# First row chunk of a SiLU feed-forward backward pass: four groups of h side by side over row slices of w1, x transposed in pairs

## Chip, cores, metric

One Trainium2 chip, one core. The metric is the device time of one execution in microseconds (us). The span in a profile is the profiled part of it; it is 1.7 to 2.0 us shorter than the time here.

## The reference, cut

```python
def _fwd_reference(x, w1, w2):          # x [1,2048,640], w1 [640,1536], w2 [1536,640], bfloat16
    h = jnp.einsum("bsd,df->bsf", x, w1)
    h = jax.nn.silu(h)
    return jnp.einsum("bsf,fd->bsd", h, w2)

def reference(x, w1, w2, grad_out):     # the output, and the gradients of x, w1, w2
    out, vjp = jax.vjp(_fwd_reference, x, w1, w2)
    return (out, *vjp(grad_out))
```

## The kernel before

The 2048 rows go in four chunks of 512. For a chunk, TensorE computes h transposed in 12 groups of 128 columns of w1, each a sum over five row blocks of 128 ("dt"). ScalarE and VectorE make silu and its derivative. Then come the down-projection, the gradient of the activation, the gradient of x, and after the last chunk the two weight gradients. Only the start of the first chunk matters here: x and w1 are loaded, x is transposed on TensorE through PSUM, and h begins.

```python
        load_x_tile(nc.sync, 0)
        load_x_tile(nc.scalar, 1)
        load_x_tile(nc.sync, 2)
        load_x_tile(nc.scalar, 3)
        for lo, hi in ((0, 2), (2, DT)):                      # FH = 256 columns
            nc.sync.dma_start(out=w1_nat[:, lo:hi, 0:FH], in_=w1_v[:, lo:hi, 0:FH])
        load_w1(FH, FC)                                       # columns 256..511
        for fc in range(1, NFC):                              # columns 512..1023, 1024..1535
            load_w1(fc * FC, (fc + 1) * FC)
        # ... loads of w2, transposing loads of grad_out, w2, w1 (cut)
        def pe_x_tile(xT, st):
            for lo, hi, copy in ((0, DS, nc.vector.tensor_copy), (DS, DT, nc.scalar.copy)):   # DS = 3
                tp = ps_h.tile([P, hi - lo, P], dt_in, name="tp", tag="hp")
                for dt_ in range(lo, hi):
                    nc.tensor.transpose(tp[:, dt_ - lo, :], x_nat[:, st, dt_ * P:(dt_ + 1) * P], ident[:])
                copy(out=xT[:, lo:hi, st * P:(st + 1) * P], in_=tp[:])
        for st in range(STC):
            pe_x_tile(xT_next, st)
        for i in range(NFILL):                                # 4 fills, reading the last x tile (cut)
            nc.tensor.matmul(wp[:, 0:P], lhsT=ident[:], rhs=x_nat[:, STC - 1, 0:P], start=True, stop=True)
        def h_group(ft, xT, aT, ghT):
            hp = ps_h.tile([P, SC], FP32, name="hp")          # 8 PSUM buffers in all
            for dt_ in range(DT):
                nc.tensor.matmul(hp[:], lhsT=w1_nat[:, dt_, ft * P:(ft + 1) * P], rhs=xT[:, dt_, :],
                                 start=(dt_ == 0), stop=(dt_ == DT - 1))
            # silu to aT, tanh, two VectorE steps to ghT (cut)
        # ... first chunk:
                for ft in range(FT):
                    h_group(ft, xT, aT, ghT)
```

Before all this, 26 matmuls on a constant run from launch until x arrives, so that the TensorE clock is raised early.

## Time and profile before

| | before |
|---|---|
| median of the three executions | 321.93 us (321.66 to 322.12) |
| span of the profiled execution | 320.5 us |
| first h matmul | 6.48 us |
| first matmul of the down-projection (60 h matmuls later) | 19.43 us |

From the page of the kernel before: span, TensorE's busy time with its share and number of instructions, the chain that ended last by engine, and the group of h matmuls (busy us, mean ns of one, idle before them and what ended it).

```profile
span 320.5 us, 3556 instructions
...
PE 314.0 (98%) x1477; PEld 145.9 (46%) x1506; DVE 101.8 (32%) x179; ACT 78.6 (25%) x142; POOL 0.7 (0%) x6
...
PE 97%; DMA 1%; issue 1%; ACT 0%; SPq 0%; DVE 0%; DVEq 0%
...
L161 PE MATMUL hp<-xT,w_nat 128*128 128x512 bf16 x232 | 56.4, 379 | 0.6 <-ACT xT L149 0.2
```

TensorE is the whole story: 98% busy, 97% of the chain. As the change keeps TensorE's matmuls, the time can only come down where TensorE waits. The timeline of the first 20 us (start, duration, engine, line, operation, output<-inputs, count, and in brackets the idle time before it and its releaser):

```profile
0.78 2.93 PE L96 MATMUL wp<-const-bfloat16-1.0 128*128 128x128 bf16 x26 [0.78 <-PEq L362]
...
3.62 0.74 PE L148 MATMUL tp<-ident,x_nat 128*128 128x128 bf16 x10
...
5.32 0.73 PE L148 MATMUL tp<-ident,x_nat 128*128 128x128 bf16 x10 [0.96 <-DMA x_nat<-in_x_dram]
...
5.81 0.65 ACT L149 COPY xT<-tp 128x256 bf16<-128x256 bf16 x2 [1.04 <-PE tp L148]
...
6.48 13.11 PE L161 MATMUL hp<-xT,w_nat 128*128 128x512 bf16 x58 [0.21 <-ACT xT L149]
7.75 0.60 ACT L168 ACTIVATE aT<-hp 128x512 bf16<-128x512 f32 x1 [1.30 <-PE hp L161]
...
19.43 10.74 PE L196 MATMUL hp<-aT,w_nat 128*128 128x512 bf16 x48
```

The reader sees the warm-up, two rounds of ten transposes, the last copy of transposed x (ScalarE, ending near 6.46), and then h without a break up to 19.43: 12.95 us for 60 matmuls, 0.216 us each. All that TensorE waits for in this execution (us in total, times, longest):

```profile
PE tp L148 <- DMA x_nat<-in_x_dram: 1.0, 1, 1.0
PE wp L96 <- PEq L362: 0.8, 1, 0.8
PE hp L161 <- ACT xT L149: 0.2, 1, 0.2
```

```profile
w_nat<-in_w_dram SPq DMA_DIRECT2D x1, 640.0 KB, 6.5
```

Issued at 1.16 and 1.19, the tiles land at 5.50 and 5.27 us. Issued at 3.16, the second block lands at 9.65, and the fifth group, its first reader, starts 20 matmuls after 6.48, at 10.80: a margin of 1.1 us in this one execution. (Landing times to the hundredth here and below are the trace's own records of each transfer.)

### The profile page before, as it was taken

What the parts mean: (1) busy time and instruction counts of PE and PEld (TensorE: products, weight loads), DVE (VectorE), ACT (ScalarE), POOL (GpSimd) and SP (SyncE); (2) the same over time, 40 slices, a digit from 0 to 9 for tenths busy, and PEclk for the clock granted to TensorE, in tenths of its full rate; (3) what the DMA queues carried; (4) which work ended last, traced back from release to release, by engine and by line L of the source; (5) the groups of instructions that cost most, each with busy time, mean ns of one, the idle gap of its engine ahead of it and who ended that gap; (6) DMA issues with size and microseconds to landing.
All of it is one profiled execution on the core that took longest, in us unless ns stands there. A gap on an engine that the chain in (4) does not pass through costs nothing.

```text
span 320.5 us, 3556 instructions
## 1 busy us (share of the span) xinstructions
PE 314.0 (98%) x1477; PEld 145.9 (46%) x1506; DVE 101.8 (32%) x179; ACT 78.6 (25%) x142; POOL 0.7 (0%) x6
## 2 busy tenths in 40 slices
PE   7999999999999999999999999999999999999996
PEld 5444444444444444444444444444444444444443
DVE  1871551477510087810147741000000100001001
ACT  3960001555201255411054520110100001001100
POOL 0000000000000000000000000000000000000000
PEclk9999999999999999999999999999999999999999
DMA  8999999999699884392445079819999999995011
GB/s 246 316 192 209 254 265 253 320 271 277 215 229 336 203 237 122 118 319 66 127 159 141 2 254 268 217 25 293 262 240 263 249 203 343 251 281 181 33 49 35
DMA packets 149264, 66.69 MB, mean 208 GB/s; under 512 B 112640, under 2 KB 149248, under 8 KB 149248
## 3 DMA queue, kind: packets, MB, share of 16 engines
q1 hardware_dynamic: 148960, 66.13, 80.8%
q10 hardware_dynamic: 288, 0.33, 0.3%
q8 instruction: 12, 0.20, 0.2%
q14 instruction: 4, 0.03, 0.0%
HBM read 9.18 MB, written 28.97 MB: 119 GB/s over the span
## 4 chain that ended last, share of the span: by engine, by line
PE 97%; DMA 1%; issue 1%; ACT 0%; SPq 0%; DVE 0%; DVEq 0%
PE hp L196 32%; PE hp L180 16%; PE hp L286 16%; PE hp L161 16%; PE hp L334 15%; DMA x_nat<-in_x_dram 1%; PE hp L316 1%; ACT xT L149 0%; PE tp L148 0%; SPq L123 0%; DVE g_2366 L327 0%; DVEq L327 0%
## 5 line engine op out<-in xcount | busy, mean ns | idle before, releaser
L161 PE MATMUL hp<-xT,w_nat 128*128 128x512 bf16 x232 | 56.4, 379 | 0.6 <-ACT xT L149 0.2
L180 PE MATMUL hp<-goT,w2T 128*128 128x512 bf16 x238 | 56.8, 379 | 0.1
L196 PE MATMUL hp<-aT,w_nat 128*128 128x512 bf16 x235 | 52.2, 379 | 0.3
L196 PE MATMUL hp<-ghT,w1T 128*128 128x512 bf16 x235 | 52.2, 379 | 0.3
L286 PE MATMUL hp<-a_blk,go_nat 128*128 128x512 bf16 x236 | 51.8, 379 | 0.2
L334 PE MATMUL hp<-gh_blk,x_nat 128*128 128x512 bf16 x219 | 48.2, 379 | 0.3
L204 ACT ACTIVATE oT<-hp 128x512 bf16<-128x512 f32 x24 | 14.3, 597 | 110.0 <-PE hp L196 110.0
L168 ACT ACTIVATE aT<-hp 128x512 bf16<-128x512 f32 x48 | 28.7, 597 | 31.7 <-PE hp L161 31.7
L196 PEld LDWEIGHTS <-w_nat 128*128 128x128 bf16 x240 | 23.5, 98 | 28.3
L180 PEld LDWEIGHTS <-w2T 128*128 128x128 bf16 x240 | 23.5, 98 | 28.3
L286 PEld LDWEIGHTS <-go_nat 128*128 128x128 bf16 x240 | 23.5, 98 | 28.3
L161 PEld LDWEIGHTS <-w_nat 128*128 128x128 bf16 x240 | 23.4, 98 | 28.4 <-issue 0.4
L196 PEld LDWEIGHTS <-w1T 128*128 128x128 bf16 x240 | 23.4, 98 | 28.4
L206 DVE CAST oT<-hp 128x512 bf16<-128x512 f32 x16 | 11.1, 692 | 78.0 <-PE hp L196 78.0
L187 DVE SCALAR_TENSOR_TENSOR ghT<-ghT,hp 128x512 bf16<-128x512 bf16 x48 | 32.5, 682 | 7.3 <-PE hp L180 7.3
L334 PEld LDWEIGHTS <-x_nat 128*128 128x128 bf16 x224 | 21.9, 98 | 26.4
L173 DVE SCALAR_TENSOR_TENSOR ghT<-aT,v 128x512 bf16<-128x512 bf16 x48 | 33.0, 688 | 0.6
L172 DVE TENSOR_SCALAR v<-t 128x512 bf16<-128x512 f32 x48 | 20.5, 427 | 29.2 <-ACT t L170 29.2
L170 ACT ACTIVATE t<-hp 128x512 f32<-128x512 f32 x48 | 28.4, 591 | 0.0
L296 DVE CAST g2T<-hp 128x512 bf16<-128x512 f32 x7 | 4.8, 692 | 46.1 <-PE hp L286 46.1
L294 ACT ACTIVATE g2T<-hp 128x512 bf16<-128x512 f32 x8 | 4.8, 598 | 47.0 <-PE hp L286 40.7
L343 ACT ACTIVATE g_2140<-hp 128x512 bf16<-128x512 f32 x1 | 0.6, 597 | 13.6 <-DMA out_dram<-g_2077 13.6
(33 smaller groups left out, 29.3 us busy)
## 6 DMA issues: line engine op xcount, KB each, us to landing
aT_scr<-aT SPq DMA_DIRECT2D x4, 1536.0 KB, 6.7
ghT_scr<-ghT SPq DMA_DIRECT2D x4, 1536.0 KB, 8.0
out_dram<-o_sb SPq DMA_DIRECT2D x8, 640.0 KB, 3.4
oT_scr<-oT SPq DMA_DIRECT2D x4, 640.0 KB, 3.9
go_nat<-in_grad_out_dram SPq DMA_DIRECT2D x4, 640.0 KB, 8.1
gxT_scr<-oT SPq DMA_DIRECT2D x4, 640.0 KB, 4.7
w_nat<-in_w_dram SPq DMA_DIRECT2D x2, 960.0 KB, 10.9
x_nat<-in_x_dram SPq DMA_DIRECT2D x3, 640.0 KB, 7.8
```

What stands on the lines that cost most here:

```text
L161: nc.tensor.matmul(hp[:], lhsT=w1_nat[:, dt_, ft * P:(ft + 1) * P], rhs=xT[:, dt_, :], start=(dt_ == 0), stop=(dt_ == DT - 1),)
L168: nc.scalar.activation(aT[:, ft, :], hp[:], ACT.Silu)
L170: nc.scalar.activation(t[:], hp[:], ACT.Tanh, scale=0.5)
L172: nc.vector.tensor_scalar(out=v[:], in0=t[:], scalar1=-0.5, scalar2=0.5, op0=ALU.mult, op1=ALU.add)
L173: nc.vector.scalar_tensor_tensor(out=ghT[:, ft, :], in0=aT[:, ft, :], scalar=1.0, in1=v[:], op0=ALU.subtract, op1=ALU.mult)
L180: nc.tensor.matmul(gp[:], lhsT=w2T[:, dt_, ft * P:(ft + 1) * P], rhs=goT[:, dt_, :], start=(dt_ == 0), stop=(dt_ == DT - 1),)
L187: nc.vector.scalar_tensor_tensor(out=ghT[:, ft, :], in0=ghT[:, ft, :], scalar=1.0, in1=gp[:], op0=ALU.add, op1=ALU.mult)
L196: nc.tensor.matmul(op_[:], lhsT=w_all[:, ft, dt_ * P:(dt_ + 1) * P], rhs=rhs_all[:, ft, :], start=(ft == 0), stop=(ft == FT - 1),)
L204: nc.scalar.activation(oT[:, dt_, :], op_[:], ACT.Copy)
L206: nc.vector.tensor_copy(out=oT[:, dt_, :], in_=op_[:])
L286: nc.tensor.matmul(gp[:], lhsT=go_nat[:, st, dt_ * P:(dt_ + 1) * P], rhs=a_blk[:, st, :], start=(st == 0), stop=(st == ST - 1),)
L334: nc.tensor.matmul(gp[:], lhsT=x_nat[:, st, dt_ * P:(dt_ + 1) * P], rhs=gh_blk[:, st, :], start=(st == 0), stop=(st == ST - 1),)
```

## The change

The intent: let h start as soon as the first row block of x is transposed and the first row slice of w1 is there, and feed it slice by slice: four groups share a slice, so four matmuls run per 128 KB. The queues and the order of the x loads are not changed by this diff.

```diff
-        for lo, hi in ((0, 2), (2, DT)):
-            nc.sync.dma_start(out=w1_nat[:, lo:hi, 0:FH], in_=w1_v[:, lo:hi, 0:FH])
-        load_w1(FH, FC)
+        for lo, hi in ((0, 1), (1, 2), (2, 3), (3, DT)):
+            nc.sync.dma_start(out=w1_nat[:, lo:hi, 0:FC], in_=w1_v[:, lo:hi, 0:FC])
         for fc in range(1, NFC):
             load_w1(fc * FC, (fc + 1) * FC)
 ...
+        def pe_x_pair(xT, st):
+            for dt_ in range(DT):
+                tp = ps_h.tile([P, 2, P], dt_in, name="tp", tag="hp")
+                for q in range(2):
+                    nc.tensor.transpose(tp[:, q, :], x_nat[:, st + q, dt_ * P:(dt_ + 1) * P], ident[:])
+                copy = nc.scalar.copy if dt_ % 2 else nc.vector.tensor_copy
+                copy(out=xT[:, dt_, st * P:(st + 2) * P], in_=tp[:])
+        pe_x_pair(xT_next, 0)
         for i in range(NFILL):
-            nc.tensor.matmul(wp[:, 0:P], lhsT=ident[:], rhs=x_nat[:, STC - 1, 0:P], ...)
+            nc.tensor.matmul(wp[:, 0:P], lhsT=warm, rhs=warm, start=True, stop=True)
+        pe_x_pair(xT_next, 2)
 ...
+        def h_first(xT, aT, ghT):                       # FB = 4, KM = 3, LAG_G = 4
+            hps = []
+            for ft in range(FB):
+                hps.append(ps_h.tile([P, SC], FP32, name="hp"))
+            for dt_ in range(KM):
+                for ft in range(FB):
+                    h_mm(hps[ft], ft, xT, dt_, dt_ + 1)
+            for i in range(FT + LAG_G):
+                if i < FT:
+                    if i < FB:
+                        h_mm(hps[i], i, xT, KM, DT)
+                    else:
+                        hps.append(ps_h.tile([P, SC], FP32, name="hp"))
+                        h_mm(hps[i], i, xT, 0, DT)
+                    silu_a(i, hps[i], aT)
+                if i >= LAG_G:
+                    silu_grad(i - LAG_G, hps[i - LAG_G], aT, ghT)
 ...
-                for ft in range(FT):
-                    h_group(ft, xT, aT, ghT)
+                h_first(xT, aT, ghT)
```

## The prediction

> **What bounds the kernel now.** TensorE. The page shows PE busy 314.0 of 320.5 us (98%) at full granted clock; the chain that ended last is 97% PE. In the timeline h runs from 6.48 to 19.43 us: 60 matmuls at 0.216 us, no gap. That is the warm gap for 512 columns in the Trainium skill, "TensorE: Matmul & The Clock Gate", section "Back-to-back issue gap"; the trace agrees. The waits view lists no later PE wait worth naming. Only the head (0 to 6.48) and the tail are not matmul-bound, and the change touches the head alone.
>
> **What sets the head.** By the landings in the trace, x tiles 0 to 3 land at 3.57, 3.74, 5.27 and 5.50 us. The last ten transposes issue from 5.32 to 5.83 (0.056 apart), four fills follow, and the last copy (ScalarE, 0.373 us) ends at 6.46. The first h matmul waits for it. w1 is not the gate: its first three pieces land at 5.78, 6.43 and 7.39, before use.
>
> **What the change does.**
> - The x loads stay as they are, queues and order. No gain.
> - w1's first 512 columns come as rows 0, 1, 2, 3-4. At the observed rate (192 KB in 0.65 us) I estimate landings near 5.8, 6.2, 6.6 and 7.4; four groups side by side need them at 6.1, 7.0, 7.8 and 8.7. It removes a w1 wait that the trace doesn't have. The next block landed at 9.65 and will be needed near 10.4; its issue moves back 0.4 us. Tight, but it holds.
> - Transposes in pairs by row block: the first h matmul needs only block 0 of all four tiles. The second transpose waits for tile 3, so nine run from 5.55 to 6.05. The copy of block 0 (VectorE, 256 columns; estimated 0.29 us from 0.358 at 384) runs 5.81 to 6.10. The other copies end before 6.7, ahead of need.
> - The fills no longer read x; the compiled order puts them behind the warm-up: off the critical path, before and after.
> - Silu of four groups first, tanh and gradient four groups later: ScalarE's 24 activations (about 13 us at their 0.54 us spacing) start near 9.3 instead of 7.75 and end near 22.5 instead of 20.7. The gradient is not used until about 32; the last silu (19.9) comes before its matmul (21.4). PSUM buffers are held longer, but eight suffice.
>
> **On the critical path:** first h matmul near 6.12 instead of 6.48: 0.36 us. The matmul count is unchanged; the rest just shifts.
>
> **Predicted time: 321.6 us, range 321.0 to 322.2.** Faster by over 2%: 0.01; within 2%: 0.98; slower: 0.01.
>
> **Right or wrong in the profile:** first h matmul between 6.0 and 6.3; its releaser a VectorE copy of xT, not w1; 60 h matmuls still in 12.95 us, no PE wait at the fifth group; ScalarE idle until about 9.3; PE busy near 314; span about 320.1.
>
> **What would make it wrong:** w1's next block landing after 10.4 (a stall of some tenths); x tile 3 slowed by the larger w1 runs; the TensorE clock, raised at 3.67 us in this trace, dropping or rising late because the fills moved (1 to 2 us); a later DMA-released stage that does not move forward with the matmuls, so that the gain is given back.

## More of the kernel before

The transfers whose issue falls in a window (KB each, us from issue to landing): x tiles 3 and 2 first, then w1's second block, columns 512 to 1023.

```profile
x_nat<-in_x_dram ACTq DMA_DIRECT2D x1, 160.0 KB, 4.3
x_nat<-in_x_dram SPq DMA_DIRECT2D x1, 160.0 KB, 4.1
```

## The result, and the profile after

The changed kernel took 322.48 us in the median of four executions (321.83 to 322.83), the kernel before 321.80 (321.54 to 322.12). The ratio is 1.0018, 95% interval 1.0000 to 1.0037. Ratios are computed from means: the mean time of one kernel's fast runs over that of the other's of the same rounds, so a ratio is not quite that of the medians quoted. The forecast was 321.6 with a range up to 322.2, so the measured median lies above the range. The class, within 2%, was right, but that was never in doubt.

The same lines of the page after:

```profile
span 320.7 us, 3592 instructions
...
PE 315.9 (98%) x1506; PEld 145.9 (45%) x1506; DVE 101.1 (32%) x181; ACT 77.8 (24%) x142; POOL 0.7 (0%) x6
...
PE 96%; DMA 3%; DVE 0%; issue 0%; DVEq 0%
...
L158 PE MATMUL hp<-xT,w_nat 128*128 128x512 bf16 x240 | 57.2, 379 | 1.2 <-DMA w_nat<-in_w_dram 1.2
```

```profile
3.50 0.50 PE L153 MATMUL wp<-const-bfloat16-1.0 128*128 128x128 bf16 x4
...
3.84 1.52 PE L147 MATMUL tp<-ident,x_nat 128*128 128x128 bf16 x20
4.15 1.54 DVE L149 COPY xT<-tp 128x256 bf16<-128x256 bf16 x6 [4.15 <-PE tp L147]
...
5.30 4.64 PE L158 MATMUL hp<-xT,w_nat 128*128 128x512 bf16 x20
...
8.68 2.06 ACT L167 ACTIVATE aT<-hp 128x512 bf16<-128x512 f32 x4 [2.97 <-PE hp L158]
...
11.13 8.81 PE L158 MATMUL hp<-xT,w_nat 128*128 128x512 bf16 x40 [1.19 <-DMA w_nat<-in_w_dram]
...
19.77 10.52 PE L221 MATMUL hp<-aT,w_nat 128*128 128x512 bf16 x48
```

```profile
PE hp L158 <- DMA w_nat<-in_w_dram: 1.2, 1, 1.2
PE wp L99 <- PEq L385: 0.8, 1, 0.8
```

```profile
x_nat<-in_x_dram ACTq DMA_DIRECT2D x1, 160.0 KB, 3.5
x_nat<-in_x_dram SPq DMA_DIRECT2D x1, 160.0 KB, 3.2
```

```profile
w_nat<-in_w_dram SPq DMA_DIRECT2D x1, 640.0 KB, 7.3
```

The head became much shorter than forecast: the first h matmul starts at 5.30 instead of 6.48. Most of that is not the pairing: x tiles 2 and 3 landed after 3.2 and 3.5 us instead of 4.1 and 4.3, so the last of them came 0.86 us earlier (4.64 instead of 5.50); the other 0.32 us lie between that landing and the first h matmul. But 20 matmuls later TensorE waits for w1's second block, which landed at 11.08 us, 7.3 after its issue, not 6.5. The bracket says 1.19 us, counted from the modelled end of the matmul before; from start to start it is 1.57, less the usual 0.22, so 1.35 us lost. Row slice 1 of w1 cost another 0.15 (landed at 6.27, needed at 6.16). The sum closes: 1.18 won, 1.35 + 0.15 lost, and the down-projection starts at 19.77 instead of 19.43, 0.34 later (0.32 by the sum). From there to the end of the span both kernels take the same: 300.9 us after, 301.0 before.

So the trace shows a new wait that eats a larger gain than was forecast. It is one execution, though. Are both figures, the early x and the late w1, the change's doing?

### The profile page after: what moved, and what is told of

It is laid out like the page before. It is cut to its first block, busy times and chain, and to the rows that moved or that the text cites. A ratio compares the mean times of both kernels' runs of the same rounds, so it can differ in the third digit from the quotient of the medians.

```text
span 320.7 us, 3592 instructions
## 1 busy us (share of the span) xinstructions
PE 315.9 (98%) x1506; PEld 145.9 (45%) x1506; DVE 101.1 (32%) x181; ACT 77.8 (24%) x142; POOL 0.7 (0%) x6
## 4 chain that ended last, share of the span: by engine, by line
PE 96%; DMA 3%; DVE 0%; issue 0%; DVEq 0%
PE hp L221 32%; PE hp L309 16%; PE hp L205 16%; PE hp L357 15%; PE hp L158 15%; DMA w_nat<-in_w_dram 2%; PE hp L339 1%; DMA x_nat<-in_x_dram 1%; DVE g L350 0%; DVEq L350 0%
## 5 line engine op out<-in xcount | busy, mean ns | idle before, releaser
L158 PE MATMUL hp<-xT,w_nat 128*128 128x512 bf16 x240 | 57.2, 379 | 1.2 <-DMA w_nat<-in_w_dram 1.2
L231 DVE CAST oT<-hp 128x512 bf16<-128x512 f32 x16 | 11.1, 692 | 76.2 <-PE hp L221 76.2
L368 DVE CAST g<-hp 128x512 bf16<-128x512 f32 x7 | 4.8, 692 | 47.0 <-PE hp L357 26.7
```

What stands on the lines that cost most here:

```text
L231: nc.vector.tensor_copy(out=oT[:, dt_, :], in_=op_[:])
```

## The experiments

Theory A: the earlier start leaves the second block too little time, so the gain in the head is paid back at the fifth group. Rival B: that wait was one execution's accident and the time goes elsewhere (silu starting later, PSUM held longer). Kernels are compared only within the same rounds.

### The two kernels again: a_again, b_again, a_again2, a_again3

No edit.

> The changed kernel unchanged, for a second trace and more rounds. Theory A (the head got about 1.2 us shorter, and the fifth group then waits for w1's second block, columns 512 to 1023): the first h matmul starts near 5.3 us again, the second block lands near 11 us again, TensorE waits 1 to 1.5 us before the fifth group, ratio to before 1.000 to 1.003. Rival B (the late landing was an accident of one execution, and the time is lost elsewhere): the second block lands near 9.7, no wait of TensorE, and the ratio is still near 1.002.

> The kernel before, unchanged, for a second trace and as a null comparison: ratio 1.000 within 0.1%. If x tiles 2 and 3 land near 5.3 and 5.5 us again, their earlier landing in the changed kernel (4.4 and 4.6) belongs to the change (theory A1: w1's larger runs behind them disturb them less); if they land near 4.5 here too, it is chance from one execution to the next (A2).

> The changed kernel once more, for a third trace beside its split version on another chip. Theory A: ratio to before 0.999 to 1.002; if the second block of w1 lands later than 4.3 us after the first h matmul, TensorE waits for exactly the difference. Rival F (the slow executions come from a late raise of the TensorE clock instead): a slow trace shows the clock raised after 6.2 us and h matmuls 0.43 us apart, as the slow execution of b_reuse did.

> A fourth trace of the changed kernel: long packets 4 us or more between 4 and 9 us (8.8, 9.8 and 10.3 so far); the fifth group waits by as much as the second block lands later than 4.3 us after the first h matmul (1.35, 0 and 0.3 us so far).

Measured: b_again 1.0000 (0.9988 to 1.0012). The changed kernel 0.9995 (0.9980 to 1.0009; 321.45 to 323.00 in six runs) and 0.9983 (0.9970 to 0.9996) on another chip, below what was expected there. a_again3 is one run: 321.53 beside 322.22 of before. The traces, in us; "needed" is the first h matmul plus 20 spacings of 0.2158 (12.95 us over 60):

| trace | last x tile lands | clock raised | first h | second block lands | needed | lost at fifth group | down-projection |
|---|---|---|---|---|---|---|---|
| before | 5.50 | 3.67 | 6.48 | 9.65 | 10.80 | 0 | 19.43 |
| b_again | 4.76 | 5.27 | 6.06 | 10.46 | 10.38 | 0.13 | 19.15 |
| changed | 4.64 | 3.73 | 5.30 | 11.08 | 9.77* | 1.35 | 19.77 |
| a_again | 4.71 | 5.49 | 5.79 | 9.27 | 10.11 | 0 | 18.74 |
| a_again2 | 4.60 | 4.39 | 5.90 | 10.49 | 10.22 | 0.30 | 19.18 |
| a_again3 | 4.54 | 4.84 | 5.67 | 9.98 | 9.99 | 0.05 | 18.67 |

(* with the 0.15 us lost at row 1 added.) The timeline of TensorE for the start and end of h, in a_again (nothing late) and in a_again2:

```profile
5.79 13.11 PE L158 MATMUL hp<-xT,w_nat 128*128 128x512 bf16 x58
18.74 1.46 PE L221 MATMUL hp<-aT,w_nat 128*128 128x512 bf16 x6
```

```profile
5.90 13.44 PE L158 MATMUL hp<-xT,w_nat 128*128 128x512 bf16 x58 [0.47 <-DMA w_nat<-in_w_dram]
19.18 1.03 PE L221 MATMUL hp<-aT,w_nat 128*128 128x512 bf16 x4
```

In a_again2 the first h matmul itself was released by w1's first slice (landed at 5.86), not by a copy of x.

What follows. The early landing of x is not the change's alone: it came early in b_again too, with the old loads, so chance (A2) is enough for it. Over all 18 traces, though, the last x tile landed after 5 us only with the old w1 pieces (before, and b_reuse below: two of four traces, against none of fourteen with the new ones). So A1, that the new pieces disturb x less, may hold for a part and stays open. The second block's landing scatters as well, 9.3 to 11.1 us for one and the same program; with the old loads it was 9.2 to 10.5 in four traces, so that the change itself makes it later is not shown. But the same lateness costs the two kernels different amounts, because the changed one needs the block up to 1 us earlier: the block at 10.46 cost b_again 0.13, at 10.49 it cost a_again2 0.30, and at 11.08 it cost 1.35. Where nothing was late (a_again), the span is 319.7. So A's wait exists but not in every execution. Whether the first four executions were a bad draw or that call was a slower one is not shown: its interval (1.0000 to 1.0037) does not meet that of a_again2 (0.9970 to 0.9996), the calls ran on different chips where the chip is recorded, and for the first it is not.

The pairing itself can be read from the distance between the last x tile's landing and the first h matmul. With the clock raised before the last transposes it is 0.98 before and 0.66 in the changed trace; with the clock raised later, 1.30 (b_again) and 1.08 (a_again). That is 0.2 to 0.3 us, close to the 0.36 forecast. Other traces below, with the clock raised before the last transposes, agree: 0.98 with the old transposes (b_w1rows2), 0.71 with pairs (a_split2, a_halves).

### Taking the wait away: a_reuse, and the same in the kernel before: b_reuse

```diff
-                        h_mm(hps[i], i, xT, 0, DT)
+                        h_mm(hps[i], i - FB if i < 2 * FB else i, xT, 0, DT)
```

Groups 4 to 7 of the first chunk read w1's first 512 columns, which landed long before; the result is wrong (relative error 0.41), work and loads are the same. b_reuse does the same in the kernel before, by an argument of `h_group`.

> Wrong result on purpose: groups 4 to 7 of the first row chunk read w1's columns 0 to 511 again, so that nothing needs the second block before group 8. Same work, same loads. Theory A: the wait of about 1.3 us is gone, the down-projection starts near 18.3 instead of 19.8 us, ratio to before 0.996 (about 320.6 us). Rival B: the ratio stays near 1.002.

> Wrong result on purpose: the kernel before with groups 4 to 7 of the first chunk reading w1's columns 0 to 511 again, so that it never waits for the second block. Theory A says that before rarely waits there (0 and 0.13 us in its two traces): ratio 0.999 to 1.000. If it gains as much as the changed kernel did by the same step (0.2%), that wait was always there and is not a price of the change.

Measured: a_reuse 0.9978 (0.9965 to 0.9990), against 0.9995 of a_again: means 321.47 and 321.96. So an estimate of what the wait costs the changed kernel is 0.5 us on average; with five and six executions of this scatter (95%: 0.5 ± 0.7) the difference is not clear of noise. The gain over the kernel before is, but it was half of what was expected from the one bad trace, as the wait is not always 1.35. In its trace the second block landed at 10.24 and no wait is left; the down-projection started at 19.02, not 18.3, since the clock was raised only at 6.06 and the transposes ran slowly:

```profile
6.06 13.12 PE L158 MATMUL hp<-xT,w_nat 128*128 128x512 bf16 x58
19.02 1.24 PE L221 MATMUL hp<-aT,w_nat 128*128 128x512 bf16 x5
```

b_reuse gained nothing: 1.0013 (0.9995 to 1.0030). So the wait is a price of the change, not one that was there before: rival B falls.

b_reuse's interval is wide because of its first run, 323.85 us, the one that was profiled. TensorE's timeline in it:

```profile
3.74 1.25 PE L148 MATMUL tp<-ident,x_nat 128*128 128x128 bf16 x10
5.68 1.25 PE L148 MATMUL tp<-ident,x_nat 128*128 128x128 bf16 x10 [0.70 <-DMA x_nat<-in_x_dram]
...
7.26 5.09 PE L162 MATMUL hp<-xT,w_nat 128*128 128x512 bf16 x19
```

The h matmuls stand 0.43 us apart up to 8.97 us, where the trace records the raise of the TensorE clock; in the other traces it came between 3.5 and 6.1. The Trainium skill, "TensorE: Matmul & The Clock Gate", Part 1 ("What's actually happening"), says that the clock is raised after a busy window of about 3.4 us, and that the window runs freely, so that the raise depends on where in it the matmuls begin. A scatter agrees with that, and so do the records: in all 18 traces the time from one change of the clock to the next is a whole multiple of 3.413 us. It is the third random quantity of the head (rival F): here the first four h matmuls lost about 0.8 us by it (0.38 to 0.43 us each instead of 0.216). Together with a late x (5.88 us) it made this execution 1.9 us longer than the mean of its five neighbours, in a kernel with the old head. Whether the changed kernel's 323.00 us run was of this kind, no trace tells.

### A smaller first piece: a_split, a_split2, a_best

```diff
-        for fc in range(1, NFC):
-            load_w1(fc * FC, (fc + 1) * FC)
+        load_w1(FC, FC + FC // 2)
+        load_w1(FC + FC // 2, 2 * FC)
+        load_w1(2 * FC, F)
```

a_best has, besides, three row slices instead of four: `((0, 1), (1, KM), (KM, DT))`.

> The second block of w1 comes as two halves of 256 columns, so the fifth group needs 320 KB less. Theory A: the wait before the fifth group shrinks to 0 to 0.4 us, as the first half lands about 1 us before the whole did; ratio 0.996 to 0.998. Rival B: no change, near 1.002.

> The split second block once more. Theory A: no wait at the fifth group, ratio 0.997 to 0.999 and 0.001 to 0.002 below the changed kernel beside it. If it equals the changed kernel within 0.0005, the first result was chance.

> Three row slices instead of four, and the second block in two halves. Theory A: as a_split2, 0.997 to 0.999; no additional gain from the earlier issue.

Measured: a_split 0.9979 (0.9966 to 0.9991), a_split2 on another chip 0.9977 (0.9965 to 0.9989), a_best 0.9982 (0.9970 to 0.9994), all correct. The means lie 0.51 us (a_split), 0.26 us (a_split2) and 0.10 us (a_best) below the changed kernel; the second is 0.0008 of it, a bit less than the 0.001 that was expected. None of the three differences is clear of noise (95%: ± 0.7, 0.4 and 0.5). TensorE's timelines of a_split and a_split2, start and end of h:

```profile
5.69 13.11 PE L159 MATMUL hp<-xT,w_nat 128*128 128x512 bf16 x58
18.64 1.67 PE L222 MATMUL hp<-aT,w_nat 128*128 128x512 bf16 x7
```

```profile
5.69 13.11 PE L159 MATMUL hp<-xT,w_nat 128*128 128x512 bf16 x58
18.63 1.67 PE L222 MATMUL hp<-aT,w_nat 128*128 128x512 bf16 x7
```

The fifth group's half landed at 8.49 and 8.37 us, needed at 10.0; no wait for w1 is left in either trace. a_split has the lowest mean of the correct kernels: ten executions on two chips, 320.97 to 322.03, mean 321.41. It gains 0.7 us, 0.2%, on the kernel before, clear of noise; that it also beats the changed kernel is likely (0.4 us, 95%: ± 0.4) and not settled. Three slices instead of four make no measurable difference.

### Making the wait longer: a_swap

```diff
-        for fc in range(1, NFC):
+        for fc in range(NFC - 1, 0, -1):
```

> The changed kernel with the second block of w1 queued behind the third: the suspected wait made about 2 us longer (the third block landed 1.9 us after the second in every trace). Theory A: the fifth group waits in every execution, 1.2 to 3.3 us; the down-projection starts near 20 to 21.5 us; ratio to the changed kernel 1.004 to 1.006. If something off this path set the time, less than 1.002.

Measured: 323.04 to 326.00 us in six runs, ratio to before 1.0069 (1.0042 to 1.0097). Against the mean of a_again2 beside it, 321.64, the mean of 324.35 is a ratio of 1.0084; the four runs with full granted clock have a mean of 323.57, a ratio of 1.0060; 1.004 to 1.006 was expected. Its trace is of one of the other two (granted clock 0.994):

```profile
5.99 4.48 PE L158 MATMUL hp<-xT,w_nat 128*128 128x512 bf16 x19
13.07 10.31 PE L158 MATMUL hp<-xT,w_nat 128*128 128x512 bf16 x39 [2.60 <-DMA w_nat<-in_w_dram]
23.22 1.03 PE L221 MATMUL hp<-aT,w_nat 128*128 128x512 bf16 x4
```

TensorE waited 2.60 us, and the 60 h matmuls took 17.2 us instead of 13: besides the wait, the matmuls after 13.07 ran at half rate, as the trace records the clock lowered at 12.74 and raised again at 16.15. The down-projection starts at 23.22, later than the 20 to 21.5 expected, for this second cost. So a late second block is paid in full, as A says, and a wait of this length can be paid a second time through the clock.

### The parts of the change by themselves: b_pairs, b_w1rows, b_w1rows2

b_pairs is the kernel before with `pe_x_pair` and the new fills, b_w1rows the kernel before with the four row slices (the first and second hunk of the diff above).

> The kernel before with the changed transposes alone (pairs by row block, fills behind the warm-up; old w1 pieces, old group order). Theory A (pairing shortens the head by about 0.3 us between tile 3's landing and the first h matmul; the other two parts are not needed for that): first h matmul 0.7 to 1.0 us after tile 3's landing where the clock has been raised by then, instead of 1.0 to 1.3; ratio 0.998 to 0.999, with waits for w1 now and then. Rival C (only the side-by-side order with row slices makes the earlier start usable): the second w1 piece, rows 2 to 4, is late for the third matmul, the wait eats the gain, ratio 1.000.

> The kernel before with the changed w1 loads alone (four row slices of 512 columns; old transposes, old group order). The first group then needs all four slices at once. If slices of one row block make the transfers stumble more (theory D): packets over 150 ns add up to 8 us or more between 4 and 9 us, as in three of the four traces of the changed loads, against 2.4 to 3.3 in the two of before, and the second block lands after 10 us. If not (chance): about 2 to 4 us. Time: ratio 1.000 to 1.003, as the first group waits some tenths for rows 3 and 4.

> A second trace of the kernel before with the sliced loads: long packets again above 4 us if the loads cause them (the first had 6.6), below 3.3 if that was chance.

Measured: b_pairs 0.9998 (0.9986 to 1.0010). In its trace the first h matmul starts 1.14 us after the last x tile (clock raised late, at 5.33), no wait, span 319.8; but its five runs do not show the gain. That fits rival C, that an earlier start alone is not usable with the old w1 pieces, but no trace of it shows that wait, so it stays open. b_w1rows: 1.0018 (1.0006 to 1.0030), slower, as expected. The reason expected was that the first group alone needs all four slices; the first trace, of the fastest of the five runs, has no such wait, and the second (b_w1rows2, one run) has it:

```profile
PE hp L160 <- DMA w_nat<-in_w_dram: 1.6, 2, 1.3
```

So slices without the side-by-side groups are a loss. That the side-by-side order is what makes them bearable is argued from this wait; no run has the order changed alone. Of theory D's two numbers b_w1rows met neither: 6.6 us of long packets instead of 8 or more, and a second block at 9.43 instead of after 10; b_w1rows2 met both (8.6 and 10.20).

### Issue time and the shape of the w1 transfers: a_three, a_one, a_halves

a_three is the changed kernel with three slices, so that the second block is the eighth transfer and not the ninth. In the changed trace the issue of the ninth waits for an x tile to land (tile 1, at 3.80, not tile 0 as the expectation says) and comes at 3.81; here it comes at 3.14. a_one loads the 512 columns in one transfer, `load_w1(0, FC)`; a_halves loads each slice in two halves of 256 columns.

> The changed kernel with three slices instead of four (row 0, rows 1 and 2, rows 3 and 4), so that the second block's issue does not wait for tile 0's completion and comes at about 3.1 us as before, not 3.8. If the later issue delays the block (theory E): it lands by about 0.5 us earlier and the ratio is 0.998. If the queue was never empty and issue time is immaterial: as the changed kernel, 0.9995 to 1.001, with or without a wait at the fifth group.

> For its trace alone: the changed kernel with w1's first 512 columns in one transfer of five row blocks (1 KB runs, no slices). If slicing by row block makes the transfers stumble (D1), packets over 150 ns between 4 and 9 us add up to 1.5 to 3.3 us, as in the four traces of the old order. If the 1 KB runs do (D2), to 4 us or more, as in the ten with slices. The first h matmul then waits for the whole block, near 7.3 us, so about 1.5 us slower.

> For its trace alone: the same row slices, each as two transfers of 256 columns (512 B runs as in the kernel before). D1 (slices): long packets add up to 4 us or more between 4 and 9 us. D2 (run length): 1.5 to 3.3 us.

Measured: a_three 0.9994 (0.9981 to 1.0007), the second block at 9.21, close to the earliest of the changed kernel's four (9.27 to 11.08); the ratio of 0.998 that theory E asks for did not come, so it is not supported. a_one: one run, 325.37 beside 322.22; the block came at 8.34 and TensorE waited 3.0 us for it. It landed 1 us later than expected, and the clock went down during the wait, as in a_swap: the trace records it lowered at 7.71 and raised at 11.13, with h matmuls 0.43 us apart in between. So it lost more than the 1.5 us expected. a_halves: one run, 322.42; the second block at 11.10, 1.0 us of wait by the waits view.

Why the block is late can be followed one step further. A 1 KB packet usually takes 0.05 us. In the changed trace three took 0.89, 1.24 and 1.73 us, from 4.47, 5.75 and 6.95 us on, nearly end to end; this looks like one DMA engine standing still most of the time from 4.5 to 8.7 us, though the records of packets don't name the engine. The Trainium skill, "DMA: Bandwidth & Descriptors", section "Why a DMA increments its semaphore by 16 and not by 1", says that a transfer counts as landed only when every engine that takes part has finished its share; the block landing at 11.08, while the others went on moving the next loads, agrees with that. The trace also records the sixteen steps, by that section one for each engine, in which a transfer's semaphore rises. In the changed trace fifteen of the second block's steps had come by 9.63 us, before the need at 9.77, and the last alone came at 11.08. In the four traces of the changed kernel half of the steps had come by 8.3 to 9.1, and the last lagged the fifteenth by 1.45, 0.03, 0.43 and 0.83 us. The late x tiles look the same: tile 3 had fifteen steps by 4.95 (before) and 4.73 (b_reuse) and the last at 5.50 and 5.88. In all four traces of the table with a loss at the fifth group the fifteenth step came before the need. So it was one late share of sixteen that made these waits, and the late x.

Packets over 0.15 us between 4 and 9 us add up, beyond 0.05 us each, to this:

| loads of w1 | traces | us |
|---|---|---|
| old pieces | before, b_again, b_pairs, b_reuse | 1.5 to 3.3 |
| four slices, second block whole | changed, a_again, a_again2, a_again3, a_reuse, a_swap, b_w1rows, b_w1rows2 | 6.6 to 10.3 |
| slices, second block in halves | a_split, a_split2, a_best | 3.7 to 5.7 |
| three slices | a_three | 5.7 |
| one transfer | a_one | 4.0 |
| slices in halves | a_halves | 7.7 |

So the new loads do stumble more (theory D), and less with the second block in halves, so a_split may help in two ways. But this sum does not tell when the block lands: a_again has 9.8 us of long packets and the earliest landing of the four (9.27), b_again 3.3 and 10.46. Neither explanation of the long packets holds alone, by one trace each: a_one is above the old range, against D1, and a_halves as well, against D2. What makes one share late remains open.

## Why the prediction was right or wrong

- **What bounds the kernel, what sets the head.** Right. TensorE's time after the first chunk's h is the same in every trace, 300.9 to 301.0 us, and only the head moved. One caution on the prediction's citation: its section gives 0.216 us as the gap of an isolated matmul, and about 0.131 us for a stream of weight loads and matmuls with 512 columns. h is such a stream and took 0.216, so the trace agrees with the formula and not with that second figure.
- **Pairing is worth 0.36 us.** Nearly right: 0.2 to 0.3 us between the last x tile and the first h matmul. The forecast start, 6.12, was missed (5.30 to 5.90) because it took x's landing at 5.50 from one trace; 4.5 to 5.0 is the usual value in this kernel's traces.
- **w1's slices arrive with slack everywhere.** Not always: a_again2's first h matmul waited for slice 0, and row 1 cost 0.15 us in the changed trace.
- **"The next block landed at 9.65 and will be needed near 10.4 ... Tight, but it holds."** This is the step that failed. The need moved to 9.8 to 10.2, and the landing is not a constant: 9.27 to 11.08 in four traces of the same program. In the changed trace the need came 0.7 us earlier than forecast (9.77, not 10.4) and the landing 1.4 us later (11.08, not 9.65), for the last of its sixteen shares. The loss was 1.35, 0, 0.30 and 0.05 us, 0.4 on average; the runs with the wait removed or eased (a_reuse, a_split, a_split2) give an estimate of 0.3 to 0.5 us, not clear of noise one by one. The prediction counted 0. It named this stall among its risks but gave it "some tenths", and its range reached 0.6 us above the forecast, less than half of what the first trace lost.
- **Silu first, tanh later, PSUM held longer: free.** Right; a_split has all of that and no wait.
- **The fills' move and the clock.** The clock's raise does vary by some us, but in the kernel before too; no trace ties it to the fills.
- **The time.** 321.6 forecast, 322.48 measured. Over all sixteen executions of the changed kernel the mean is 321.94, with a standard deviation of 0.53, against 322.10 and 0.29 for the 27 of the kernel before. In executions where the second block is late the fifth group gives the head's gain back, in part or whole: with the wait removed or eased the changed kernel is 0.2% faster than before, with it the three calls say 1.0018, 0.9995 and 0.9983. The first four executions had a mean of 322.40, 0.6 us above that of the other twelve; their own traces but one are not kept, so how much of this is the wait is not known. A range of 0.6 us on either side, drawn from a kernel with half that scatter, was too narrow.

## What to carry to other kernels

When a stage is started earlier, recompute the deadline of every load behind it, and compare it with the scatter of that load's landing over several traces, not with its landing in one. A margin of some tenths on a DMA that took 6 to 7 us is no margin. Where the next consumer needs only part of a transfer, try cutting the transfer there: with one block halved the change paid 0.2%, with it whole it paid between -0.2% and 0.2%.

## What the Trainium skill lacked or had wrong

- "TensorE: Matmul & The Clock Gate", "What you observe", gives the raise of the clock as ±500 ns from run to run. With warm-up matmuls from 0.78 us on, it came at 3.5 to 6.1 us in 17 traces and at 8.97 in one, where the first h matmuls lost about 0.8 us. (The page speaks of sustained activity; here TensorE waited for x after the warm-up.)
- The same page, "Why this matters for your kernels", asks for no idle gaps over about 3 us. A wait of 2.6 us was enough in one trace here (a_swap: clock lowered from 12.74 to 16.15 us); in a_one it was a wait of 3.0.
- The same page, Part 4, says that the raised clock does not engage for transposes. Transposes stood 0.056 us apart once it was raised (kernel before, 0.51 us for nine steps) and 0.107 before that (b_reuse). The records call them MATMUL and don't show the transpose mode itself.
- No page tells how much the landing of one transfer scatters: 640 KB of w1 landed at 9.27 to 11.08 us in four traces of one program, and single 1 KB packets took up to 1.73 us, where 0.05 is usual. Nor does one tell how far a single share of the sixteen can lag: 0.03 to 1.45 us behind the fifteenth in these four.
